# First loads whole and in another order, x^T copied in three pieces, two columns of ones, joint key products from tile 2

## Chip, cores, metric

One core of one Trainium2 chip. The metric is the device time of one execution in microseconds (us). A fast run is one that the measurement did not class as disturbed; only fast runs enter ratios. The time of an execution is some 1.3 us longer than the span of the program in its trace.

## The reference

Two linear-attention blocks, A and B, on one x, mixed by a gate. x is 2048 x 640, bfloat16, with 32 heads of 20.

```python
qkv = (x @ wqkv)...                       # for A and for B
phi = lambda t: where(t > 0, t + 1, exp(t)) + 1e-6
pq, pk = phi(q), phi(k)
kv = einsum("bhsd,bhse->bhde", pk, v); z = sum of pk over s
o  = (pq . kv) / (pq . z + 1e-6);  a = o @ wo
g  = sigmoid((x * gate_w).sum(-1));  out = g * a + (1 - g) * b
```

Only the first of the kernel's stages matters here: the keys, k = x @ wk for 16 tiles of 128 rows, for A and B. Each product needs a piece of x^T (640 = 5 chunks of 128) and the chunk of wk that belongs to it.

## The kernel before

The program is a list of operations with data dependencies. A small list scheduler orders them per engine; `after` chains the operations of TensorE in the order written. Cuts are marked `# ...`.

```python
# loads: SP is SyncE, ACT is ScalarE; both issue DMAs
for eng, h in (("SP", 0), ("ACT", 1)):
    dma(eng, "xn0_%d" % h, XN[:, 0, HALF*h : HALF*h+HALF], ..., writes=[("XN0", h)])
load_wk("ACT", 0); load_wk("SP", 1); load_x("ACT", 1)
load_wk("SP", 2); load_wk("ACT", 3); load_wk("SP", 4)
for c0, c1 in ((0, 1), (1, 3), (3, 5)):
    dma("SP", "wkB%d" % c0, WK["B"][:, c0:c1, :], ...)
for t0, t1 in ((2, 4), (4, 8), (8, 12), (12, 16)):      # x^T of the other tiles, by the DMA
    dma("SP", "xt%d" % t0, XT[:, :, 128*t0 : 128*t1], xin[128*t0 : 128*t1, :], transpose=True)
# ... x, wv, wo, wq

def transpose_x(t):          # x^T of tiles 0 and 1, by TensorE
    tt = _Tile(1)            # one PSUM bank; five transposes, then two copies
    # ...
    for c0, c1 in ((0, 2), (2, NC)):
        sch.op("DVE", lambda e: e.tensor_copy(XT[:, c0:c1, ...], PSB[:, tt.banks[0], ...]), ...)

warm(6)                      # dummy products of constants, 512 columns each
transpose_x(0); warm(1); first("A", (0, 0), (0, 1))      # (tile, chunk)
transpose_x(1); warm(1); first("A", (1, 0), (1, 1))
first("A", (0, 2), (1, 2), (0, 3), (1, 3))
for t in (0, 1):
    first("A", (t, 4)); phi_k("A", t, kt["A", t])
for X, ts in (("B", (0, 1)), ("A", (2, 3)), ("B", (2, 3))):
    for t in ts:
        first(X, *[(t, c) for c in range(NC)]); phi_k(X, t, kt[X, t])
for t in range(4, NT):
    k_both(t)                # A and B together: products of 512, 512 and 256 columns
```

Of the kernel before, what the change touches and what calls it, by code (L numbers as in the profile page):

```python
# [15 lines left out]
ACT = mybir.ActivationFunctionType  # L16
# [3 lines left out]
D = 640  # L20
H = 32
DH = 20
NT = 16
NB = 4
NC = 5
EPS = 1e-6
HALF = 320
# [263 lines left out]
def _dve_ns(n, rate=1):  # L291
    return n / (0.96 * rate) + 68.0
# [6 lines left out]
def bass_gated_mix__linear_attn_block__linear_attn_block__prompt_kernel(nc, A_x, A_wqkv, A_wo, B_x, B_wqkv, B_wo, gate_w, out):  # L299
    cap = nc.inline_tensor(_build_consts(), name="kconsts").ap().bitcast(dt.bfloat16)  # L300
    xin = A_x[0]
    wqkv = {"A": A_wqkv, "B": B_wqkv}
    wo = {"A": A_wo, "B": B_wo}
    XS = ("A", "B")

    with ExitStack() as es:
        E = es.enter_context

        def sb(name, shape, dtype=dt.bfloat16):
            return E(nc.sbuf_tensor(name, shape, dtype))  # L310

        XN = sb("XN", [128, NT, XW])
# [37 lines left out]
        IDN = sb("IDN", [128, 128])  # L350

        PS = E(nc.psum_tensor("ps", [128, 8, 512], dt.float32))
        PSB = PS[:, :, :].rearrange("p b f -> p (b f)").bitcast(dt.bfloat16).rearrange("p (b f) -> p b f", f=1024)
# [3 lines left out]
        sch = _Sched()  # L357

        def pair(t, n):
            b0, b1 = t.banks  # L360
            return PS[:, b0 : b1 + 1, 0:n]

        def dma(eng, name, dst, src, reads=(), writes=(), us=1.0, transpose=False, slow=False):
            n_sem[0] += 1
            sem = E(nc.semaphore(name="d%d_%s" % (n_sem[0], name)))

            def fn(e):
                if slow:
                    with nc.allow_non_contiguous_dma(reason="few elements"):
                        ins = e.dma_start(dst, src)  # L370
                else:
                    ins = e.dma_start(dst() if callable(dst) else dst, src() if callable(src) else src, transpose=transpose)  # L372
                return ins.then_inc(sem, 16)

            return sch.op(eng, fn, us * 1e3, reads=reads, writes=writes, name=name, sem=sem)
# [12 lines left out]
        def weights(X, lo, c0, c1):  # L388
            return wqkv[X][128 * c0 : 128 * c1, lo : lo + D].rearrange("(c p) f -> p c f", p=128)
# [18 lines left out]
        def load_x(eng, t):  # L408
            dma(eng, "xn%d" % t, XN[:, t, 0:D], xin[128 * t : 128 * t + 128, :], writes=[("XN", t)], us=0.25)

        def load_wk(eng, c):
            dma(eng, "wkA%d" % c, WK["A"][:, c, :], weights("A", D, c, c + 1)[:, 0, :], writes=[("WK", "A", c)], us=0.25)

        for eng, h in (("SP", 0), ("ACT", 1)):
            dma(
                eng, "xn0_%d" % h, XN[:, 0, HALF * h : HALF * h + HALF], xin[0:128, HALF * h : HALF * h + HALF],
                writes=[("XN0", h)], us=0.15,
            )
        load_wk("ACT", 0)
        load_wk("SP", 1)  # L420
        load_x("ACT", 1)
        load_wk("SP", 2)
        load_wk("ACT", 3)
        load_wk("SP", 4)
        for c0, c1 in ((0, 1), (1, 3), (3, 5)):
            dma(
                "SP", "wkB%d" % c0, WK["B"][:, c0:c1, :], weights("B", D, c0, c1), writes=[("WK", "B", c) for c in range(c0, c1)],
                us=0.55 * (c1 - c0),
            )
        for t0, t1 in ((2, 4), (4, 8), (8, 12), (12, 16)):  # L430
            dma(
                "SP", "xt%d" % t0, XT[:, :, 128 * t0 : 128 * t1], xin[128 * t0 : 128 * t1, :],
                writes=[("XT", t) for t in range(t0, t1)], us=0.82 * (t1 - t0), transpose=True,
# [3 lines left out]
        for t0, t1 in ((2, 4), (4, 8), (8, 12), (12, 16)):  # L437
            dma(
                "SP", "xn_%d" % t0, XN[:, t0:t1, 0:D], xin[128 * t0 : 128 * t1, :].rearrange("(t p) f -> p t f", p=128),
                writes=[("XN", t) for t in range(t0, t1)], us=0.5 * (t1 - t0),  # L440
# [8 lines left out]
            dma("SP", "wo5" + X, W5[(X == "B") * 64 : (X == "B") * 64 + 40, :], wo[X][600:D, :], writes=[("W5", X)], us=0.2)  # L449
            dma("SP", "wq" + X, WQ[X][:, :, :], wsrc(X, 0), writes=[("WQ", X)], us=2.6)  # L450

        sch.op("POOL", lambda e: e.memset(XN[:, :, D : D + 1], 1.0), 200, writes=[("XN1",)], name="ones")
        for X in XS:
            sch.op("POOL", lambda e, X=X: e.memset(WV[X][:, NC * D :], 0.0), 200, writes=[("WVP", X)], name="wvp" + X)

# [1 line left out]
        at = [None]  # L457

        def ones(n):
            return nc.const_aps.tensor(1.0, [128, n], dt.bfloat16)  # L460

        def warm(n):
            for _ in range(n):
                at[0] = mms(
                    "warm", lambda: [(PS[:, wt.banks[0], :], ones(128), ones(512), True, True, None)], [], [(wt,)], 1024, after=at[0],
                )


        def transpose_x(t):
            tt = _Tile(1)  # L470

            def fn(pe):
                ins = None
                for c in range(NC):
                    ins = pe.transpose(PSB[:, tt.banks[0], 128 * c : 128 * c + 128], XN[:, t, 128 * c : 128 * c + 128], IDN[:, :])  # L475
                return ins

            at[0] = sch.op(
                "PE", fn, 5 * 112, reads=[("XN", t), ("ID",)] + [("XN0", h) for h in (0, 1)][: 2 - 2 * min(t, 1)], writes=[(tt,)], name="xpose%d" % t, lat=190, after=at[0]
            )  # L480
            for c0, c1 in ((0, 2), (2, NC)):
                sch.op(
                    "DVE",
                    lambda e, c0=c0, c1=c1: e.tensor_copy(  # L484
                        XT[:, c0:c1, 128 * t : 128 * t + 128],
                        PSB[:, tt.banks[0], 128 * c0 : 128 * c1].rearrange("p (c f) -> p c f", f=128),
                    ),
                    _dve_ns(128 * (c1 - c0)), reads=[(tt,)], writes=[("XTC", t, c) for c in range(c0, c1)], name="xev%d" % t,
                )
# [3 lines left out]
        def phi_k(X, t, tile):  # L493
            es = _Tile(1, ring["ek"])

            def ek():
                return EK[:, es.slot, :]

            def ek2():
                return ek().rearrange("p (h f) -> p h f", f=HALF)  # L500

            sch.op(
                "ACT", lambda e: e.activation(ek2(), pair(tile, HALF), ACT.Exp),
                _act_ns(D), reads=[(tile,)], writes=[(es,)], name="ek%s%d" % (X, t),
            )
            sch.op(
                "DVE", lambda e: e.tensor_scalar(ek(), ek(), 1.0, EPS, op0=ALU.min, op1=ALU.add), _dve_ns(D, 4),
                reads=[(es,)], writes=[(es,)], name="tk%s%d" % (X, t),
            )
            sch.op(  # L510
                "DVE",
                lambda e: e.scalar_tensor_tensor(
                    out=PK[X][:, t, :].rearrange("p (h f) -> p h f", f=HALF), in0=pair(tile, HALF), scalar=0.0,
                    in1=ek2(), op0=ALU.max, op1=ALU.add,
                ),
                _dve_ns(D), reads=[(tile,), (es,)], writes=[("F", X, "k", t)], name="sk%s%d" % (X, t),
            )
# [69 lines left out]
        def g_unit(X, k):  # L587
            tile = _Tile(2)

            def steps(lo, hi):  # L590
                r = []
                for t in range(lo, hi):
                    w = PK[X][:, t, k : D : NC]
                    r.append((PS[:, tile.banks[0], 0:HALF], w, XN[:, t, 0:HALF], t == 0, t == NT - 1, None))
                    r.append((PS[:, tile.banks[1], 0 : HALF + 1], w, XN[:, t, HALF : D + 1], t == 0, t == NT - 1, None))
                return r

            for lo, hi in ((0, NT - 4), (NT - 4, NT)):
                gone[X] = mms(
                    "g%s%d_%d" % (X, k, lo), lambda lo=lo, hi=hi: steps(lo, hi),  # L600
                    [("F", X, w, t) for w in ("k", "k5") for t in range(lo, hi)] + [("XN", t) for t in range(lo, hi)] + [("XN1",)],
                    [(tile,)], (hi - lo) * (D + 13),
                )
            sch.op(
                "ACT", lambda e: e.activation(GS[:, k, :].rearrange("p (h f) -> p h f", f=HALF), pair(tile, HALF), ACT.Copy),  # L605
                _act_ns(D), reads=[(tile,)], writes=[("GS", k)], name="gs%s%d" % (X, k),
            )
            sch.op(
                "DVE", lambda e: e.tensor_copy(Z32[X][:, k : k + 1], PS[:, tile.banks[1], HALF : HALF + 1]), 80,
                reads=[(tile,)], writes=[("Z", X, k)], name="z%s%d" % (X, k),  # L610
            )
            dma(
                "SP", "gt%s%d" % (X, k), GT[X][:, :, k, :], GS[:, k, :], reads=[("GS", k)], writes=[("GT", X, k)], us=1.6,
                transpose=True,
            )
# [265 lines left out]
                    ))  # L881


        kt = {(X, t): _Tile(2) for X in XS for t in range(4)}

        def first(X, *tc):
            for t, c in tc:
                k_part(X, t, kt[X, t], [c], chain=True)

        warm(6)  # L890
        transpose_x(0)
        warm(1)
        first("A", (0, 0), (0, 1))
        transpose_x(1)
        warm(1)
        first("A", (1, 0), (1, 1))
        first("A", (0, 2), (1, 2), (0, 3), (1, 3))
        for t in (0, 1):
            first("A", (t, 4))
            phi_k("A", t, kt["A", t])  # L900
        for X, ts in (("B", (0, 1)), ("A", (2, 3)), ("B", (2, 3))):
            for t in ts:
                first(X, *[(t, c) for c in range(NC)])
                phi_k(X, t, kt[X, t])
        for t in range(4, NT):
            k_both(t)
        for k in range(NC):
            g_unit("A", k)
# [82 lines left out]
```

## Time and profile before

| | before |
|---|---|
| time, median of 3 (and of 6 with the next 3) | 191.21 us (191.18) |
| span in the trace | 190.2 us |
| TensorE busy | 98% |
| first key product; unbroken stream from | 4.52 us; 6.81 us |
| joint products from | tile 4, 17.1 us |

The page of the profile of before: busy time per engine (with its share of the span and the number of instructions), then the chain that ended last.

```profile
PE 186.1 (98%) x1291; PEld 125.5 (66%) x1300; DVE 129.5 (68%) x269; ACT 76.3 (40%) x127; POOL 8.2 (4%) x14
...
PE 95%; DMA 2%; issue 0%; ACTq 0%; DVE 0%; ACT 0%
```

TensorE (PE) is both the busiest engine and nearly the whole chain. No other engine can give time back; only TensorE's idle or slow stretches can.

The timeline of TensorE in before, first 20 us. Columns: start, length, engine, line, operation, output and inputs, shape, count, and in brackets the idle time before it and what ended it.

```profile
0.77 2.72 PE L383 MATMUL ps<-const-bfloat16-1.0 128*128 128x512 bf16 x6 [0.77 <-PEq L976]
3.29 0.73 PE L475 MATMUL ps<-IDN,XN 128*128 128x128 bf16 x5
3.82 0.63 PE L383 MATMUL ps<-const-bfloat16-1.0 128*128 128x512 bf16 x1
4.52 1.12 PE L383 MATMUL ps<-WK,XT 128*128 128x320 bf16 x4
5.97 0.45 PE L475 MATMUL ps<-IDN,XN 128*128 128x128 bf16 x5 [0.33 <-DMA XN<-in_A_x_dram]
6.26 0.38 PE L383 MATMUL ps<-const-bfloat16-1.0 128*128 128x512 bf16 x1
6.81 13.42 PE L383 MATMUL ps<-WK,XT 128*128 128x320 bf16 x91 [0.17 <-DVE XT L484]
```

Read it so. The first five transposes take 0.73 us, the second five 0.45: the same work at half and at full clock. The starts of single instructions in the trace say it exactly: transposes 107 ns apart, later 56; products of 320 columns 267 ns apart, later 136. At 5.97 us TensorE had waited for tile 1 of x, at 6.81 us for VectorE's copy of its transpose. From there the stream has no stall.

### The profile page before, as it was taken

To read this page: it belongs to the slowest core of one execution; us is meant where nothing else is said; L and a number is where in the kernel's file an instruction comes from. 1 tells how busy PE (TensorE), PEld (TensorE's weight loads), DVE (VectorE), ACT (ScalarE), POOL (GpSimd) and SP (SyncE) were. 2 spreads that over 40 slices of the span, in tenths; PEclk is the share of its full clock that TensorE was granted. 3 is DMA by queue.
4 is the path that set the end of the run, shared out by engine and by line. 5 is a ranking of instruction groups with operands and counts; after the bars stand their busy time and mean duration, and the time that the engine had idled before them with its cause. 6 is when DMAs were issued, how large, how long until landed. Compare 5 with 4: busy or idle time off the path is not lost.

```text
span 190.2 us, 3207 instructions
## 1 busy us (share of the span) xinstructions
PE 186.1 (98%) x1291; PEld 125.5 (66%) x1300; DVE 129.5 (68%) x269; ACT 76.3 (40%) x127; POOL 8.2 (4%) x14
## 2 busy tenths in 40 slices
PE   8899999999999999999999999999999999999995
PEld 3576555555788888888855666455556677777774
DVE  1198989898700008997169997899999959833324
ACT  2155565556311111203255478565553513331332
POOL 8900000000000000000000000000000000000000
DMA  5999699991011111111134004666000173221212
GB/s 166 327 236 177 216 389 363 327 229 34 0 37 35 34 34 38 34 38 34 34 78 118 3 23 172 164 221 172 0 0 3 41 228 94 90 72 45 72 69 69
DMA packets 32080, 21.49 MB, mean 113 GB/s; under 512 B 16834, under 2 KB 31810, under 8 KB 32066
## 3 DMA queue, kind: packets, MB, share of 16 engines
q1 hardware_dynamic: 31490, 20.72, 39.2%
q10 hardware_dynamic: 576, 0.57, 0.9%
q8 instruction: 10, 0.16, 0.3%
q14 instruction: 4, 0.03, 0.1%
HBM read 12.05 MB, written 5.31 MB: 91 GB/s over the span
## 4 chain that ended last, share of the span: by engine, by line
PE 95%; DMA 2%; issue 0%; ACTq 0%; DVE 0%; ACT 0%
PE ps L383 95%; DMA XN<-in_A_x_dram 2%; ACTq L372 0%; PE ps L475 0%; ACT TS L864 0%; DVE OL L870 0%; DVE XT L484 0%
## 5 line engine op out<-in xcount | busy, mean ns | idle before, releaser
L383 PE MATMUL ps<-WK,XT 128*128 128x512 bf16 (+2 forms) x256 | 43.9, 331 | 0.5 <-DVE XT L484 0.2
L383 PE MATMUL ps<-XN,FE 128*128 128x320 bf16 x320 | 44.3, 300 | 0.0
L383 PEld LDWEIGHTS ps<-XN,FE 128*128 128x128 bf16 x320 | 37.5, 117 | 6.0
L383 PEld LDWEIGHTS ps<-WK,XT 128*128 128x128 bf16 x260 | 25.4, 98 | 19.1 <-DVE XT L484 1.1
L748 ACT ACTIVATE EK<-ps 128x512 bf16<-128x512 f32 x40 | 23.9, 597 | 18.4 <-PE ps L383 17.9
L757 DVE SCALAR_TENSOR_TENSOR FE<-ps,EK 128x512 bf16<-128x512 f32 x40 | 26.8, 686 | 0.7
L864 ACT ACTIVATE TS<-ps,GA 128x640 f32<-128x640 f32 (+2 forms) x18 | 13.2, 735 | 29.6 <-PE ps L383 29.6
L383 PE MATMUL ps<-WPB,FE 128*128 128x320 bf16 (+1 forms) x165 | 24.7, 295 | 0.0
L383 PE MATMUL ps<-WPA,FE 128*128 128x320 bf16 (+1 forms) x165 | 24.7, 295 | 0.0
L568 ACT ACTIVATE EK<-ps 128x512 bf16<-128x512 f32 (+1 forms) x36 | 18.3, 526 | 13.8 <-PE ps L383 13.8
L870 DVE SCALAR_TENSOR_TENSOR OS<-ps,GA,TS 128x640 bf16<-128x640 f32 x15 | 13.0, 868 | 15.2 <-PE ps L383 12.8
L383 PE MATMUL ps<-XT,WQB 128*128 128x512 bf16 x99 | 22.5, 379 | 0.1
L383 PE MATMUL ps<-XT,WQA 128*128 128x512 bf16 x96 | 22.2, 379 | 0.3 <-issue 0.2
L605 ACT ACTIVATE GS<-ps 128x640 bf16<-128x640 f32 x10 | 7.0, 704 | 37.1 <-PE ps L383 37.1
L578 DVE SCALAR_TENSOR_TENSOR FE<-ps,EK 128x512 bf16<-128x512 f32 (+1 forms) x36 | 20.5, 597 | 0.4
L383 PEld LDWEIGHTS ps<-WPA,FE 128*128 128x128 bf16 x165 | 15.9, 98 | 6.1
L383 PEld LDWEIGHTS ps<-WPB,FE 128*128 128x128 bf16 x165 | 15.8, 98 | 6.2 <-ACT TS L864 0.4
L383 PEld LDWEIGHTS ps<-XT,WQA 128*128 128x128 bf16 x100 | 11.6, 118 | 9.4 <-issue 0.4
L383 PEld LDWEIGHTS ps<-XT,WQB 128*128 128x128 bf16 x100 | 11.7, 117 | 9.2
L710 DVE SCALAR_TENSOR_TENSOR GP<-XN,GWB 128x640 bf16<-128x640 bf16 x16 | 13.2, 828 | 4.1 <-PE ps L383 3.5
L816 DVE TENSOR_TENSOR FE<-FE,RX 128x1280 bf16<-128x1280 bf16 (+1 forms) x20 | 12.6, 683 | 1.0 <-DMA RX<-factor 1.0
L752 DVE TENSOR_SCALAR EK<-EK 128x512 bf16<-128x512 bf16 x40 | 10.8, 286 | 2.5 <-ACT EK L748 1.8
(52 smaller groups left out, 87.8 us busy)
## 6 DMA issues: line engine op xcount, KB each, us to landing
out_dram<-OS SPq DMA_DIRECT2D x15, 160.0 KB, 1.8
XN<-in_A_x_dram SPq DMA_DIRECT2D x3, 640.0 KB, 8.1
factor<-RC SPq DMA_DIRECT2D x4, 256.0 KB, 2.6
RX<-factor SPq DMA_DIRECT2D x4, 256.0 KB, 3.1
WVA<-in_A_wqkv_dram SPq DMA_DIRECT2D x1, 800.0 KB, 10.6
WQA<-in_A_wqkv_dram SPq DMA_DIRECT2D x1, 800.0 KB, 12.0
WVB<-in_B_wqkv_dram SPq DMA_DIRECT2D x1, 800.0 KB, 11.3
WQB<-in_B_wqkv_dram SPq DMA_DIRECT2D x1, 800.0 KB, 12.3
```

The costliest lines, as they stand in the source:

```text
L383: ins = pe.matmul(o, l, r, start=a, stop=z, tile_position=tp, skip_group_check=True)
L568: "ACT", lambda e, ps=ps, ek=ek: e.activation(ek(), ps(), ACT.Exp), _act_ns(n), reads=[(tile,)], writes=[(es,)],
L578: return e.scalar_tensor_tensor(out=out, in0=two(ps()), scalar=0.0, in1=two(ek()), op0=ALU.max, op1=ALU.add)
L605: "ACT", lambda e: e.activation(GS[:, k, :].rearrange("p (h f) -> p h f", f=HALF), pair(tile, HALF), ACT.Copy),
L710: lambda e, t=t: e.scalar_tensor_tensor(out=GP[:, :], in0=XN[:, t, 0:D], scalar=1.0, in1=GWB[:, :], op0=ALU.mult, op1=ALU.mult, accum_out= ...
L748: "ACT", lambda e: e.activation(ek(), PS[:, tile.banks[0], :], ACT.Exp), _act_ns(512), reads=[(tile,)],
L752: "DVE", lambda e: e.tensor_scalar(ek(), ek(), 1.0, EPS, op0=ALU.min, op1=ALU.add), _dve_ns(512, 4),
L757: lambda e: e.scalar_tensor_tensor(out=dst, in0=PS[:, tile.banks[0], :], scalar=0.0, in1=ek(), op0=ALU.max, op1=ALU.add),
L816: return e.tensor_tensor(out=v, in0=v, in1=RX[:, xs.slot, 512 * x + w * j : 512 * x + w * j + w].unsqueeze(1).to_broadcast([128, NC, w]), ...
L864: "ACT", lambda e, acc=acc, t_ap=t_ap: e.activation(t_ap(), acc(), ACT.Copy, scale=GA[:, 0, t : t + 1]),
L870: lambda e, acc=acc, t_ap=t_ap, o_ap=o_ap: e.scalar_tensor_tensor(out=o_ap(), in0=acc(), scalar=GA[:, 1, t : t + 1], in1=t_ap(), op0=ALU.m ...
```

## The change

Its intent is to bring the stream forward. Tile 1 of x is loaded earlier; the copies of x^T start after one or two transposes, not after five; a useful product takes the place of each dummy. The joint form of the key products begins at tile 2, and the gram product (pk^T [x, 1]) gets a second column of ones, so that it has 322 columns and not 321.

```diff
-        for eng, h in (("SP", 0), ("ACT", 1)):
-            dma(eng, "xn0_%d" % h, ...)          # halves of tile 0
+        load_x("SP", 0)
         load_wk("ACT", 0)
-        load_wk("SP", 1)
-        load_x("ACT", 1)
+        load_x("SP", 1)
+        load_wk("ACT", 1)
 ...
-        memset(XN[:, :, D : D + 1], 1.0)
+        memset(XN[:, :, D : D + 2], 1.0)
 ...
-            tt = _Tile(1)                        # five transposes, one bank
-            for c0, c1 in ((0, 2), (2, NC)):
+            for c0, c1 in ((0, 1), (1, 3), (3, NC)):
+                tt = _Tile(1)                    # own bank, own transposes, own copy
 ...
-        warm(6)
+        warm(7)
         transpose_x(0)
-        warm(1)
-        first("A", (0, 0), (0, 1))
+        first("A", (0, 0))
         transpose_x(1)
-        warm(1)
-        first("A", (1, 0), (1, 1))
-        first("A", (0, 2), (1, 2), (0, 3), (1, 3))
+        first("A", (0, 1), (1, 0), (1, 1), (0, 2), (1, 2), (0, 3), (1, 3))
 ...
-        for X, ts in (("B", (0, 1)), ("A", (2, 3)), ("B", (2, 3))):
-            for t in ts:
-                first(X, *[(t, c) for c in range(NC)])
-                phi_k(X, t, kt[X, t])
-        for t in range(4, NT):
+        for t in (0, 1):
+            first("B", *[(t, c) for c in range(NC)])
+            phi_k("B", t, kt["B", t])
+        for t in range(2, NT):
             k_both(t)
```

## The prediction

> **What bounds the kernel now.** The chain of waits gives 95% of the 190.2 us span to TensorE matmuls. From 6.81 us on, their starts in the trace follow each other every 136 ns (320 columns) or 216 ns (512) without a stall. So time can be won only before 6.81 us, or by a shorter pitch. The timeline of the start:
> - six dummies, 427 ns apart (half clock), from 0.77 us; transposes of tile 0 from 3.29 us, 107 ns apart (half clock)
> - a dummy; at 4.52 us four key products, 267 ns apart
> - idle until tile 1 of x lands at 5.92 us (the chain names this load: 4.28 us)
> - transposes from 5.97 us, 56 ns apart (full clock), a dummy that fills the wait for VectorE's copy (0.30 us), the stream at 6.81 us.
>
> The Trainium skill ("TensorE: Matmul & The Clock Gate", The HAM clock gate) says that the array runs at half clock until some 3.4 us of sustained activity; the trace agrees: 267 ns per 320 columns until about 5.3 us, 136 ns later.
>
> **What the change does.**
> - *Loads.* Tile 1 of x is now second on SyncE, not third on ScalarE: complete with 640 KB landed, not 800 KB. From the packets of before (0.33 MB by 3.2 us, 0.65 MB by 4.5 us, semaphores 0.3 to 0.5 us later) I estimate tile 0 at 3.6 us (before: 3.16) and tile 1 at 5.0 to 5.2 us. The seventh dummy lasts until 3.72 us and covers the later tile 0.
> - *Copies.* With three PSUM banks a copy starts after its own transposes. The product of tile 0, chunk 1 needs nothing new and hides tile 1's first copy: the 0.55 us from dummy to stream becomes two useful products.
> - *Joint K from tile 2.* Forty products of 320 columns (5.44 us) become 20 x 216 + 10 x 109 ns = 5.41 us. VectorE and ScalarE keep up in the twelve joint tiles of before; I expect no new wait. The transposed load of tiles 2 and 3 landed at 10.06 us; it will be needed at about 10.7.
> - *Two ones columns.* 160 products of 321 columns (137 ns) become 322: within 0.1 us in all. The wider memset is off the path.
> - Everything after the keys is issued in the same order.
>
> **On the critical path.** Tile 1 lands some 0.8 us earlier and some 0.3 us of dummy and copy wait go, against two products left over for the stream (0.27 us, perhaps at half clock). The product of tile 0, chunk 2, at 7.35 us before, I expect at 6.2 to 6.6. Gain 0.9 us, kept to the end, since nothing later waits for anything but TensorE.
>
> **Prediction.** 190.3 us, 8 in 10 within 189.8 to 190.9. Faster by over 2%: 0.01; within 2%: 0.98; slower by over 2%: 0.01.
>
> **What shows each step.** Tile 0's transposes at 3.7 to 3.8 us, not waiting for x; tile 1's near 5.1 us, and no gap in the stream from there; joint products at 216/109 ns from tile 2; gram products still at 136 to 137 ns; every later landmark (gram products at 49.6 us, end) earlier by the same 0.9 us.
>
> **What would make it wrong.** Whole rows in two queues share the DMA engines, so tile 0 could come after 3.8 us and push all; without the dummies the clock could stay low past 5.4 us, which would cost 0.3 to 1 us; weight chunk 2 or 3 could be the new last wait (I estimate 5.9 to 6.4 us, needed at 6.2); VectorE, fuller in joint tiles, could hold PSUM banks.

## The result

| | before | changed | ratio, 95% interval |
|---|---|---|---|
| 6 runs each | 191.18 us (191.08 to 191.43) | 190.78 us (190.08 to 191.15) | 0.9973 (0.9955 to 0.9991) |

A ratio is the mean time of one kernel's fast runs over the mean of the other's in the same rounds, so not quite the ratio of the medians. The gain is 0.5 us here, small but clear of noise; 0.9 was forecast, and 190.78 lies in the range. Two things ask for a reason: the gain is short of the forecast, and the changed kernel's runs spread over 1.1 us where before's spread over 0.35.

The page of the changed kernel, same lines as before:

```profile
PE 186.2 (98%) x1289; PEld 124.2 (66%) x1289; DVE 130.2 (69%) x275; ACT 76.5 (40%) x129; POOL 8.2 (4%) x14
...
PE 94%; DMA 3%; SPq 1%; issue 0%; ACT 0%; DVE 0%
```

Its timeline of TensorE, first 12 us (L471 is the transpose):

```profile
0.77 3.15 PE L383 MATMUL ps<-const-bfloat16-1.0 128*128 128x512 bf16 x7 [0.77 <-PEq L967]
3.80 0.71 PE L471 MATMUL ps<-IDN,XN 128*128 128x128 bf16 x5
4.40 0.62 PE L383 MATMUL ps<-WK,XT 128*128 128x320 bf16 x2
4.86 0.44 PE L471 MATMUL ps<-IDN,XN 128*128 128x128 bf16 x5
5.14 2.88 PE L383 MATMUL ps<-WK,XT 128*128 128x320 bf16 x20
8.22 0.72 PE L383 MATMUL ps<-WK,XT 128*128 128x320 bf16 x4 [0.20 <-DMA WK<-in_B_wqkv_dram]
9.17 3.15 PE L383 MATMUL ps<-WK,XT 128*128 128x320 bf16 x19 [0.24 <-DMA WK<-in_B_wqkv_dram]
```

And the chain that ended last, its last steps (start, length, what):

```profile
3.53 5.59 DMA WK<-in_B_wqkv_dram
9.12 0.05 issue
9.17 177.87 PE ps L383 x1241
187.04 0.02 issue
187.07 0.40 ACT TS L859
187.47 0.03 issue
187.50 0.38 DVE OL L865
```

The front went better than forecast. The product of tile 0, chunk 2 started at 5.95 us, against 7.36 before: 1.41 us won. Then 0.76 us were given back. The stream waited at 8.22 us for B's weight chunks 1 and 2, which landed at 8.17, and at 9.17 us for chunks 3 and 4, which landed at 9.12 (0.36 and 0.40 us more than the usual distance between starts; the brackets show less because the modelled ends of products reach into the gap). In before the same loads landed at 7.99 and 8.85 us and were needed later. A load lands in 16 parts. Of chunks 1 and 2, 15 parts had landed by 7.38 us and the last at 8.17; the product was due at 7.86, so this wait hung on one part. The chain now leads not to x but to the last load of B's weights. 1.41 - 0.76 = 0.65 us, and the span fell by 0.64, from 190.18 to 189.54.

Everything after the keys moved by that amount: the gram products start at 48.94 us against 49.59. The joint products kept their distances of 216 and 109 ns. The gram products of 321 columns were 137.0 ns apart on average, those of 322 are 136.9.

So theory W: **the stream now overtakes B's key weights, and their landing sets its pace.** The rival, theory C: **the clock of TensorE rises at a moment that changes from run to run; before hid much of a late rise behind its wait for x, and the changed kernel does not.** One trace can't decide it: in this one the clock was full from 4.86 us, early. The Trainium skill says of the clock's window ("TensorE: Matmul & The Clock Gate", The HAM clock gate) that it is free-running and that the count of slow products therefore varies from run to run.

### The profile page after: what moved, and what is told of

It reads as the page before. It is cut to its first block, busy times and chain, and to the rows that moved or that the text cites. A ratio compares the mean times of both kernels' runs of the same rounds, so it can differ in the third digit from the quotient of the medians.

```text
span 189.5 us, 3208 instructions
## 1 busy us (share of the span) xinstructions
PE 186.2 (98%) x1289; PEld 124.2 (66%) x1289; DVE 130.2 (69%) x275; ACT 76.5 (40%) x129; POOL 8.2 (4%) x14
## 4 chain that ended last, share of the span: by engine, by line
PE 94%; DMA 3%; SPq 1%; issue 0%; ACT 0%; DVE 0%
PE ps L383 94%; DMA WK<-in_B_wqkv_dram 3%; SPq L372 1%; ACT TS L859 0%; DVE OL L865 0%
## 5 line engine op out<-in xcount | busy, mean ns | idle before, releaser
L383 PEld LDWEIGHTS ps<-WK,XT 128*128 128x128 bf16 x250 | 24.1, 98 | 19.9 <-DMA WK<-in_B_wqkv_dram 1.1
L563 ACT ACTIVATE EK<-ps 128x512 bf16<-128x512 f32 (+1 forms) x42 | 21.4, 526 | 16.2 <-PE ps L383 16.2
L573 DVE SCALAR_TENSOR_TENSOR FE<-ps,EK 128x512 bf16<-128x512 f32 (+1 forms) x42 | 23.9, 597 | 0.5
L383 PE MATMUL ps<-XT,WQA 128*128 128x512 bf16 x100 | 22.8, 380 | 0.0
L567 DVE TENSOR_SCALAR EK<-EK 128x512 bf16<-128x512 bf16 (+1 forms) x42 | 11.4, 271 | 3.1
```

Source lines behind the costliest of these rows:

```text
L383: ins = pe.matmul(o, l, r, start=a, stop=z, tile_position=tp, skip_group_check=True)
L563: "ACT", lambda e, ps=ps, ek=ek: e.activation(ek(), ps(), ACT.Exp), _act_ns(n), reads=[(tile,)], writes=[(es,)],
L567: "DVE", lambda e, ek=ek: e.tensor_scalar(ek(), ek(), 1.0, EPS, op0=ALU.min, op1=ALU.add), _dve_ns(n, 4),
L573: return e.scalar_tensor_tensor(out=out, in0=two(ps()), scalar=0.0, in1=two(ek()), op0=ALU.max, op1=ALU.add)
```

## The experiments

Twelve kernels, four to a chip; each group of four has runs of before on its chip beside it (fast ones 190.95 to 191.64, 191.22 to 191.97 and 191.08 to 191.61 us, so before spreads by 0.5 to 0.75 us there).

### Chunk order for B (two runs)

```diff
-        for t in (0, 1):
-            first("B", *[(t, c) for c in range(NC)])
-            phi_k("B", t, kt["B", t])
+        first("B", *[(t, c) for c in range(NC) for t in (0, 1)])
+        for t in (0, 1):
+            phi_k("B", t, kt["B", t])
```

> The changed kernel, with the products of B for tiles 0 and 1 issued chunk by chunk (0 of both tiles, 1 of both tiles, ...) and not tile by tile, so that each chunk of B's key weights is needed later. Theory W (B's weights are the new last wait: 0.36 us for chunks 1 and 2, 0.40 us for chunks 3 and 4 in the changed kernel's trace): both gaps vanish, joint products start near 10.3 us and not 11.08, time 0.6 to 0.8 us below the changed kernel, about 190.1 us, and the spread of the runs narrows. Rival C (the gain fell short because the clock of TensorE rises later in most unprofiled runs, now that dummies are gone): the gaps are not the cost, time stays at 190.6 to 190.9 us and the spread of 1 us stays.

Measured: 190.56 us (190.19 to 190.98), ratio to before 0.9963 (0.9948 to 0.9977). The 0.6 to 0.8 us did not appear (0.9963 here, 0.9973 for the changed kernel, on another chip), so theory W alone falls; the time is also just under theory C's range, and the spread was 0.8 us. The trace had no wait for B, but two for A: for chunk 2 (0.40 us at 6.71 us: its first of 16 parts landed at 4.61, its 15th at 5.47, its last at 6.66) and for chunk 3 (0.14 us at 7.40 us). The clock was still low at 5.38 us:

```profile
5.38 1.09 PE L383 MATMUL ps<-WK,XT 128*128 128x320 bf16 x6
6.71 5.54 PE L383 MATMUL ps<-WK,XT 128*128 128x320 bf16 x35 [0.24 <-DMA WK<-in_A_wqkv_dram]
```

Later, beside the changed kernel on one chip:

> Chunk order for B again, beside the changed kernel on this chip. As the clock and the landings both vary, the 0.5 us that it gained with late loads should show only in part: 0.1 to 0.4 us below the changed kernel; equal if late rises of the clock dominate these runs.

Measured: 190.05 us (189.81 to 191.11), ratio 0.9945 (0.9922 to 0.9969); the changed kernel of the same rounds had 0.9958 (0.9946 to 0.9970). The order is hinted to be better, not shown.

### The changed kernel again (two runs)

No edit.

> The changed kernel word for word, for a second trace and beside the next three on one chip. Both theories: about 190.8 us with a spread near 1 us. Theory W: its trace shows a wait for B's key weights (or for a late chunk of A's) before the joint products start. Theory C: the clock of TensorE in its trace rises at another moment than 4.6 us.

Measured: 190.67 us (190.12 to 191.02), ratio 0.9948 (0.9931 to 0.9965), with before at 191.51 on that chip. The profiled execution took 190.12 us.

> The changed kernel again, beside the others on this chip: 0.5 to 1.0 us below before, spread near 1 us. The trace: a rise of the clock somewhere between 4.2 and 7.6 us, and waits for B's weights only if its last chunks land after about 8.6 us.

Measured: 190.51 us (190.27 to 190.77), ratio 0.9958 (0.9946 to 0.9970). The profiled execution took 190.77 us. The repeats spread over 0.90 and 0.50 us, before over 0.75 and 0.53 beside them: the contrast of 1.1 and 0.35 us in the runs on record did not return.

With the run on record that makes three traces of one kernel, and they show three states. The timeline of the first repeat:

```profile
3.75 0.72 PE L471 MATMUL ps<-IDN,XN 128*128 128x128 bf16 x5
4.36 0.71 PE L383 MATMUL ps<-WK,XT 128*128 128x320 bf16 x2
4.87 0.49 PE L471 MATMUL ps<-IDN,XN 128*128 128x128 bf16 x5
5.20 7.06 PE L383 MATMUL ps<-WK,XT 128*128 128x320 bf16 x46
```

and of the second:

```profile
3.77 0.71 PE L471 MATMUL ps<-IDN,XN 128*128 128x128 bf16 x5
4.37 0.71 PE L383 MATMUL ps<-WK,XT 128*128 128x320 bf16 x2
4.88 0.74 PE L471 MATMUL ps<-IDN,XN 128*128 128x128 bf16 x5
5.41 3.87 PE L383 MATMUL ps<-WK,XT 128*128 128x320 bf16 x24
```

Neither waits for a weight, though theory W had expected a wait in the first. The clock rises at another moment than on record in both, as theory C had expected. In the first the second set of transposes takes 0.49 us (full clock from 4.97 us), in the second 0.74 (half clock until 6.2 us). The table of windows shows the same as counts, for 5.00 to 6.80 us (columns: window, length, busy time and number of instructions of PE, PEld, DVE, ACT and POOL, granted clock, DMA share, GB/s). First repeat:

```profile
5.00:6.80 1.80, 1.80 (x18) 1.29 (x17) 0.62 (x3) 0.00 (x0) 1.80 (x1) 1.00 1.07 367
```

Second repeat:

```profile
5.00:6.80 1.80, 1.80 (x13) 1.31 (x12) 0.72 (x3) 0.00 (x0) 1.80 (x1) 1.00 1.06 370
```

Both are 100% busy, with the same granted clock in the table (1.00), and yet 18 transposes and products fall into the one and 13 into the other. Busy time and the clock column do not tell the two apart; the counts and the starts do. So does a record of the clock that nine of the fourteen packed traces hold and `prof` does not list: full from 4.96 us in the first repeat, from 6.32 us in the second. The traces of before and of the changed kernel on record hold none; there the starts alone speak.

| trace of the changed kernel | full clock from | last of B's chunks landed | waits for weights | joint products from | time |
|---|---|---|---|---|---|
| on record | before 4.86 us | 9.12 us | 0.76 us | 11.08 us | 190.84 us |
| first repeat | 4.96 us | 8.41 us | none | 10.37 us | 190.12 us |
| second repeat | 6.32 us | 8.43 us | none | 11.02 us | 190.77 us |

The starts of the joint products differ by 0.72 and 0.66 us from the best, the times by 0.72 and 0.65. In one trace the weights explain it, in the other the clock: half speed from 4.96 to 6.32 us costs 0.68 us by this estimate.

### Only the clock

The transposes and the first forty products read constants, and tiles 2 and 3 read the x^T of tiles 0 and 1. The result is wrong on purpose.

```diff
-   pe.transpose(PSB[...], XN[:, t, 128*c : 128*c+128], IDN[:, :])
+   pe.transpose(PSB[...], ones(128), IDN[:, :])
-   (PS[...], XT[:, c, xc], WK[X][:, c, HALF*h : HALF*h+HALF], ...)
+   (PS[...], XT[:, c, xc], ZR[:, :], ...)          # ZR: 0.01 throughout, memset at the start
 def k_both(t):
-   xc = slice(128*t, 128*t + 128)
+   u = t - 2 if t < 4 else t
+   xc = slice(128*u, 128*u + 128)
```

> Wrong result on purpose. The changed kernel, with the transposes and the first forty products reading constants, and tiles 2 and 3 reading the x^T of tiles 0 and 1: no wait for a load before 10 us, all loads still running. Only the clock can vary. If the clock rises anywhere between 4.2 and 7.6 us[...], the joint products start between 10.1 and 11.7 us. Theory C: runs spread over 1 us or more, between 189.7 and 191.2 us, mean near 190.4. Theory W alone (loads make the spread and the loss): all runs within 0.3 us of each other, near 189.8 us.

Measured: 189.66, 189.84, 189.89, 190.55, 190.85 and 191.00 us; mean 190.30. The spread of 1.3 us is there although no load can hold the front, and within 0.04 us it keeps to the limits expected. Theory W alone is out: with the loads taken away the runs spread as much. The trace, of the run with 190.85 us, shows half clock until 6.45 us:

```profile
4.85 0.74 PE L473 MATMUL ps<-IDN,const-bfloat16-1.0 128*128 128x128 bf16 x5
5.38 5.88 PE L383 MATMUL ps<-ZR,XT 128*128 128x320 bf16 x38
11.10 1.24 PE L383 MATMUL ps<-WK,XT 128*128 128x512 bf16 x5
```

The other five runs have no trace, so that the clock made their differences is inferred. It is large enough: the fastest is 1.19 us shorter, which at half speed asks for a rise 2.4 us earlier, at about 4.1 us (an estimate), and the trace of the run below with joint products from tile 4 has its rise at 4.07 us.

### Only the loads (two runs)

All loads wait for GpSimd's first long memset, which ends at 4.4 us, and sixteen dummies leave time for the clock to rise before x lands (their starts go from 427 to 220 ns apart near 4.8 us in one trace and 5.7 us in the other; x landed from 7.41 us).

```diff
 def dma(eng, name, dst, src, reads=(), ...):
+    reads = list(reads) + [("GATE",)]       # written by the memset of WO of A
 ...
-        warm(7)
+        warm(16)
```

> The changed kernel with all loads held back by 3.7 us (behind GpSimd's first long memset) and sixteen dummies instead of seven, so that the clock is full in every run before x lands: only the loads can vary. About 194.4 us. Theory W: the trace shows full-clock products from the first, and waits for B's chunks of 0.7 us or more; the runs spread about 1 us, as the landings of B's last chunks did (8.4 to 9.7 us in six traces). Theory C: the spread falls to 0.4 us or less.

> The same with B's products chunk by chunk. Theory W: with the clock out of the way the chunk order gains all that it promised, 0.6 to 0.7 us below the late-loads run. If the waits for B's weights are not what holds the stream: within 0.2 us of it.

Measured, with four runs each: 193.96, 193.97, 194.34 and 194.65 us in the order of the change; 193.50, 193.56, 193.67 and 193.92 us in chunk order. (The absolute times are some 3.6 us worse by construction.) The timeline of the first:

```profile
8.28 0.44 PE L472 MATMUL ps<-IDN,XN 128*128 128x128 bf16 x5
8.56 3.47 PE L384 MATMUL ps<-WK,XT 128*128 128x320 bf16 x24
12.30 2.94 PE L384 MATMUL ps<-WK,XT 128*128 128x320 bf16 x18 [0.27 <-DMA WK<-in_B_wqkv_dram]
```

With full clock throughout (0.44 us for five transposes) the wait for B's last chunks is still there, 0.43 us in this trace, and the runs spread over 0.7 us. Theory W had asked for waits of 0.7 us and a spread of 1 us, theory C for 0.4 us of spread: the size lies between, but the wait is there, so theory C alone is out as well. In chunk order the runs don't overlap with these, if only by 0.04 us and with four runs each: the means differ by 0.57 us (0.6 to 0.7 expected), and the spread is 0.42. Its trace had no wait for B and one of 0.36 us for a chunk of A:

```profile
8.62 0.98 PE L384 MATMUL ps<-WK,XT 128*128 128x320 bf16 x6
9.79 5.38 PE L384 MATMUL ps<-WK,XT 128*128 128x320 bf16 x36 [0.19 <-DMA WK<-in_A_wqkv_dram]
```

The chunk order removes what it was meant to remove. In the normal kernel its gain is not shown; of the changed kernel's three traces two had no wait for it to remove.

### The parts of the change

**Loads of before, the rest changed.**

```diff
-        load_x("SP", 0); load_wk("ACT", 0); load_x("SP", 1); load_wk("ACT", 1)
+        # halves of tile 0 on SP and ACT; wk 0 on ACT, wk 1 on SP, tile 1 third on ACT
```

> The changed kernel with the loads of before (tile 0 of x in halves on two queues, tile 1 third on ScalarE). Theory W: tile 1 lands at 5.9 us again, the stream starts near 6.25 us with two products more to do than before, product (tile 0, chunk 2) at about 7.07 us instead of 7.35, no wait for B's weights, as chunk 1 of B is needed at about 9.0 us and there at 8.0: 0.3 us below before, about 190.9 us. Rival C: the same or slower than before, 191.2 us or more, with a spread of 1 us.

Measured: 190.84, 191.11, 191.24, 192.69, 193.23 and 193.57 us, ratio 1.0044 (0.9999 to 1.0089). The first three are where theory W has them. The other three are 1.5 to 2.3 us above the slowest of these, and they make up the ratio above 1. One of them has a granted clock of 0.991 in its record, as have two runs of before on these chips (194.31 and 194.08 us, both slow); the other two read 1.0. No trace fell on such a run, so their cause stays open. The trace of a good one shows tile 1 landing at 5.45 us, 0.9 us later than with the new loads on record, and 0.5 us earlier than the same load in before.

**Copies and dummies of before, the rest changed** (the seventh dummy at the start kept), alone and together with chunk order.

```diff
-            for c0, c1 in ((0, 1), (1, 3), (3, NC)):     # three banks
+            for c0, c1 in ((0, 2), (2, NC)):             # one bank
 ...
-        first("A", (0, 0)); transpose_x(1); first("A", (0, 1), (1, 0), ...)
+        warm(1); first("A", (0, 0), (0, 1)); transpose_x(1); warm(1); first("A", (1, 0), ...)
```

> The changed kernel with x^T copied in two pieces from one bank and a dummy after each transpose, as before (seventh dummy at the start kept). Theory W: the stream starts some 0.3 to 0.5 us later, but the landing of B's chunks 3 and 4 near 9.1 us still sets the rest: within 0.1 us of the changed kernel, about 190.8 us, the waits for B's weights shorter. If the copies' share adds to the time as I costed it blind, it is 0.3 to 0.5 us slower, 191.1 to 191.3.

> Both: products of B chunk by chunk, and the old copies with dummies. Theory W: with the wait for B's weights gone the copies' share shows: 0.3 to 0.5 us above the run with chunk order alone, about 190.5 us. If the copies are worth nothing in themselves: equal to it.

Measured: 190.92 us, ratio 0.9989 (0.9970 to 1.0008), and 191.16 us, ratio 0.9987 (0.9974 to 1.0001). Without the new copies neither is clearly faster than before. Against chunk order on the same chip (0.9963) the second is 0.0024, or 0.46 us, slower, as expected. The first missed: theory W had it within 0.1 us of the changed kernel, but its mean of 191.06 is 0.50 us above that of chunk order on its chip, and its ratio is above all three of the changed kernel. That the wait for B's weights does not swallow the copies' share in most runs is suggested, not shown: the intervals overlap with that of the run on record. The first's trace is of its slowest run: the clock rose only at 6.49 us, and the stream began at 7.00 us and met no wait:

```profile
5.87 0.74 PE L471 MATMUL ps<-IDN,XN 128*128 128x128 bf16 x5
6.41 0.42 PE L383 MATMUL ps<-const-bfloat16-1.0 128*128 128x512 bf16 x1
7.00 7.22 PE L383 MATMUL ps<-WK,XT 128*128 128x320 bf16 x45 [0.17 <-DVE XT L480]
```

**Joint products from tile 4 and one column of ones, the rest changed.**

> The changed kernel with joint key products from tile 4 only and one column of ones, as before. Both theories: these two parts are worth nothing, within 0.1 us of the changed kernel of the same rounds; separate products 136 ns apart, gram products of 321 columns 137 ns apart. If joint products relieve or burden VectorE: a wait of TensorE between 10 and 17 us in the trace, and a difference of 0.2 us or more.

Measured: 190.62 us, ratio 0.9964 (0.9951 to 0.9978), beside 0.9958 for the changed kernel of the same rounds: the same within noise. These two parts are worth nothing measurable. The front is that of the changed kernel, and its trace is a fourth view of it: by the starts, the clock was full from 4.07 us, and the stream waited 0.23 us for chunk 2 of A (landed 5.97 us) and 0.29 us for B's last chunks (8.72 us). So the wait for B came back in one of three further traces of this front.

### B's chunks as single loads

Chunk order, B's weights as five loads, A's last chunk on ScalarE.

```diff
-        load_wk("SP", 4)
-        for c0, c1 in ((0, 1), (1, 3), (3, 5)):
+        load_wk("ACT", 4)
+        for c0, c1 in ((0, 1), (1, 2), (2, 3), (3, 4), (4, 5)):
```

> Chunk order for B, and B's five weight chunks as five loads, A's last chunk moved to ScalarE: each wait is for 160 KB, not 320. Same bytes in the same order. If chunk order still waits for the pairs (0.36 us for one in the late-loads trace), up to 0.2 us below chunk order alone; the rise of the clock, which this cannot move, keeps the spread near 1 us. If the extra issue on SyncE delays the transposing load: equal to it or slower.

Measured: 190.50 us (190.26 to 191.32), ratio 0.9963 (0.9947 to 0.9980). Not better than chunk order. The trace waited for A's chunks 3 and 4 (landed 6.89 and 7.72 us; 0.37 and 0.28 us), not for B. Chunk 4 is the one that the edit moved; in the changed kernel it landed at 6.06 to 6.76 us.

No version beats the changed kernel clearly. The chunk order costs nothing measurable and helped where the clock was out of the way (four runs against four).

## Why the prediction was right or wrong

The time, 190.78 us, is inside 189.8 to 190.9, the direction is right, and the gain of 0.9 us is close to the second and third sets (1.0 and 0.8 us, from ratios 0.9948 and 0.9958) and nearly twice the first (0.5). Part of the hit is luck: in the trace the front gained 0.5 us more than forecast, and waits that were not forecast took back 0.76. Step by step:

- *"Time can be won only before 6.81 us."* Right: gram products, joint products and tail kept their lengths; the start alone moved.
- *"I estimate tile 0 at 3.6 us and tile 1 at 5.0 to 5.2 us."* The mis-sized term. Tile 0 landed at 3.75 us, tile 1 at 4.55 us. In this trace 776 KB had arrived by 4.5 us, in before 658 KB: the estimate took its rate from that one trace of before. The half rows at its start are at most part of the difference, as the trace with before's loads had 730 KB by then. That the two queues share what moves the data, as the prediction has it, fits the packets: SyncE's moved 207 KB in the 1 us from 3.5 us, beside 172 of ScalarE's, and 520 KB in the 1.5 us from 6.0 us, when ScalarE's loads were done. So "the product of tile 0, chunk 2, I expect at 6.2 to 6.6" came at 5.95.
- *"Tile 1's near 5.1 us, and no gap in the stream from there."* The first half was early by 0.24 us. The second failed in the trace: two gaps, 0.76 us. The repeats show no such gap, so it holds in some executions only. The list of risks named weight chunk 2 or 3 of A as the new last wait; I had not checked B's, which in before had landed 1.27 us (chunks 1 and 2: 7.99, needed at 9.26) and 0.96 us (chunks 3 and 4: 8.85, needed at 9.81) ahead of need, while the stream was moved forward by 1.4. The named risk, a late chunk of A, did come in three other traces with these loads (chunk order, single loads, joint products from tile 4).
- *"Without the dummies the clock could stay low past 5.4 us, which would cost 0.3 to 1 us."* The cost was right for the second repeat, 0.66 us; the 1.3 us between the extremes with no load waits is more. That taking the dummies away caused it is not shown. The rise came at different moments in the traces, also of the two versions that kept the dummies (6.49 and 5.65 us by the clock record). The prediction puts the half-clock phase at some 3.4 us; in before the dummies began at 0.77 us and products were still 267 ns apart at 5.28, which is 4.5 us. That a late rise cost before less, as it waited for x until 5.92 us anyway, is argued from its timeline alone; its smaller spread did not return in the later sets.
- *Copies.* Right in size as a net gain, but the sum then took the two left-over products (0.27 us) off again. From the first transpose of tile 1 to the product of tile 0, chunk 2, before took 1.39 us and the changed kernel 1.10, these two products included: 0.30 us net. With the 1.11 us by which these transposes started earlier that makes the 1.41. With chunk order the copies and dummies measured 0.46 us.
- *Joint products, second column, needed time of the x^T of tiles 2 and 3.* Right: nothing measurable; landed at 10.31 us, needed at 11.08. In the first repeat it landed at 10.19 us and was needed at 10.37, so only 0.2 us is left there.
- *"Kept to the end."* Right: 0.65 us at the gram products and 0.64 at the end.

The gain of any single run is the front's gain of up to 1.4 us less what a late chunk or a late clock takes back. Which of the two held each of the unprofiled runs cannot be read from their times; that both occur, each without the other, is shown by the three traces, and the two isolating experiments show that each is enough to cost time.

## What to carry to other kernels

When you pull a stream forward, list all loads that it will need and by how much each landed ahead; the next one in line becomes the wait, and the margin must also cover how much landings vary from run to run. A wait near the start can also hide part of TensorE's half-clock phase (argued here, not isolated): once it is gone, the moment at which the clock rises shows in the time, so look at several traces before you explain the difference of one. Order products that share late data so that each piece is needed as late as possible (here: chunk by chunk over two tiles, 0.57 us where only the loads counted).

## What the Trainium skill lacked or had wrong

- "TensorE: Matmul & The Clock Gate", PE-mode transpose, says that the full clock does not engage for transposes. Here it does: five transposes of 128 columns started 107 ns apart while the clock was low and 56 ns apart after it rose. Dummies and products ran between them, so whether transposes alone would raise it no run here shows.
- The same page, Back-to-back issue gap, gives about 131 ns as the sustained distance of 512-column products in a stream of weight loads and matmuls, and says that its formula of some 216 ns over-counts. Here each of 140 such products had its own weight load, and they started 216 ns apart.
- The same page, The HAM clock gate, on the free-running window: the traces agree. Dummies ran from 0.77 us in all; the rise was seen by 4.07 us in one trace and not before 6.45 us in another. In eight traces with a clock record the full clock lasts 184.32 us, in the ninth 187.73: the difference, 3.41 us, is the length that the page gives for the window. The page calls the ramp under 1% of a typical span; here it spread the times by 1.3 us of 190 (0.7%) where no load was waited for, more than the change was worth.
- On no page that I read: the granted clock in the profile's table of windows was 1.00 from 5.00 to 6.80 us in the second repeat while products started 267 ns apart until 6.2 us. The clock record begins only with the rise, at 6.32 us there, and five of fourteen traces have none, so the early half-clock phase itself is visible only in the starts.
- "DMA: Bandwidth & Descriptors", Latency and other measured facts, tells of slower DMA engines for descriptors that GpSimd writes. Loads issued by SyncE and ScalarE had late parts as well: the 16 parts of one 160 KB load landed between 4.61 and 6.66 us in one trace, 15 of them by 5.47, and within 0.42 us of each other in another. Which engine carried the late part the traces do not say.
- On no page that I read: the transposing load behind B's last weights landed 1.1 to 1.2 us after them in eleven of the twelve traces of kernels with normal loads (before: 8.85 and 10.06 us; the first run in chunk order: 9.65 and 10.85 us), whenever they came. In the twelfth, the first repeat, it was 1.8 us.
